# The one-hot table's operations at other places of the attention's steps

## The chip, the cores and the metric

The kernel runs on one core of one Trainium2 chip. The metric is the device time of one execution in microseconds (us), as the median of several runs. The core's engines are named as in the profile: PE (matrix products and transpositions), DVE (vector operations), ACT (activations and copies), POOL (a second vector engine), SP (issues most DMAs). Each engine takes its instructions in the order in which they were written, and waits where a semaphore is not there yet.

## The reference

Eight batches of eight-head attention over 576 positions with head size 64 (four heads with a local mask, four with a strided one) give 4608 rows of 512; each row goes to one of eight experts, the one with the largest gate logit.

```python
scores = np.where(masks, scale * q @ k.T, -1e9)
attn = exp(scores - max) / (sum + 1e-9);  x = (attn @ v) as rows of B*S by 512
logits = x @ w_gate;  e_idx = argmax(logits);  gate_w = softmax(logits)[e_idx]
eom = sigmoid(x @ w_output_gate)
for e in range(8):
    m = e_idx == e
    out[m] = gate_w[m] * eom[m, e] * (relu(x[m] @ w1[e]) @ w2[e])
```

## The kernel before, in words

**The attention** (lines 173 to 888) is a software pipeline of 40 steps: batch b has five chunks of positions, and pass t of the loop brings in chunk t % 5 of batch t // 5. "Step 2" below is a pass with t % 5 = 2. Chunks 0 to 2 are strided, 3 and 4 local. The order on every engine is the order in which this loop writes. One pass does, for chunks of different age: on PE the scores of the new chunk (`scores`, L262 and L267), transpositions of the probabilities of the chunk two passes old (`turn_p`, L320), the products with V of the chunk three passes old (`values`, L335 and L338), and transpositions of the output of the chunk four passes old (`turn_x`, L384). DVE divides the output by its sums (`norm`, L348, L350, L353), then adds the mask to the new scores (`bar`, "the mask" below, L280 and L285) and takes the row maxima (`top`, L294). POOL subtracts the maxima (`shift`, "the subtraction", L309). ACT copies the transposed output of the pass before out of PSUM (`evac_x`, L393, L399), then the transposed probabilities (`evac_p`, L326), V tiles (L233), and last takes the exponential of the new chunk (`expo`, L313). The scores, the products with V and both kinds of transposition have one PSUM buffer each.

**The gate.** When all chunks of a batch are transposed, `logits` multiplies them with the gate's weights in two halves (L416), ACT copies the result (L420), PE transposes it (L425, "the logits' transpositions") and DVE sums it (L427). In the trace the sum of the first half ("the first sum") comes ahead of step 0's division, that of the second ("the second sum") ahead of step 1's mask. `gating` then finds each row's expert (`oh`, one-hot over the experts), counts rows (`cum`), and gives every row a slot: PE forms running numbers (L561 to L566), DVE picks the row's own one (L618) and sums it to `slots` (L621), and `lo` is the slot's low seven bits (L673).

**The one-hot table.** From `lo` and `slots` POOL makes `pos` (L676 to L678) and, with a subtraction from a row of constants, a table `hit` of 128 low numbers and 48 pages for each of six groups of rows: `low` in two pieces (L683), `high` (L686). DVE compares the whole table with zero in place (L691), so that it is one-hot ("the compare"). POOL also splits the row's weight into three bf16 `parts` (L649, L651) and multiplies the pages with five values, two for the row's number and three for the weight, into `named` (L656, "the five products"). Last PE multiplies `hit` with `named` in one PSUM tile (`place`, L662, "the placement"), and DVE adds that to a book of all rows (`enter`, L669; L671 for the first batch).

**What sets the order.** `gating` and `logits` are generators that the pass calls at nine points (`pump(1)` to `pump(9)`). `yield n` lets n further points go by; `yield 0, p` goes on at point p of the same or the next pass. Point 9 stands ahead of the mask, points 1 and 2 in the division, points 3 and 4 behind the subtraction, points 5 to 8 at the end of the pass. Batches 0 to 5 run in this way (`steady`); batches 6 and 7 are worked off in the attention's tail, in the other branch.

After the fourth batch's book entry two more chains begin: `pick` chooses the expert with the most rows, SP loads its number and starts four loads of its first weights (`ahead`, L167), and POOL fetches rows for it (L158), at fixed steps. After the attention's tail the experts follow (lines 890 to 1270), mostly PE products.

Of the kernel before, what the change touches and what calls it, by code (L numbers as in the profile page):

```python
# [20 lines left out]
E = 8  # L21
# [4 lines left out]
R = S // STRIDE  # L26
QB = 96
# [27 lines left out]
HB = CLEAR // 128  # L55
WP = 3
# [4 lines left out]
def attn_moe_kernel(  # L61
# [111 lines left out]
    def attention():  # L173
        with ExitStack() as actx:
# [364 lines left out]
            def gating(b, j0, j1, ci):  # L539
# [12 lines left out]
                def output_logit():  # L552
                    V.tensor_tensor(out=dd[:, 2], in0=oh, in1=l[:, :, E:2 * E], op=ALU.mult)
# [23 lines left out]
                def sigmoid():  # L577
                    nc.scalar.activation(out=f[:, 4, :], in_=f[:, 3, :], func=AF.Exp, scale=-1.0)
# [12 lines left out]
                yield 0  # L591
                if steady:
# [5 lines left out]
                    yield 0, 9  # L598
                    output_logit()
                    yield 0  # L600
                    output_sum()
                    yield 0
                    sigmoid()
                else:
# [10 lines left out]
                V.tensor_tensor(out=cum[0:QB, ci + 1, :], in0=cum[0:QB, ci, :], in1=s8, op=ALU.add)  # L615
                yield 0 if steady else 1
                dst = slots[:, tcols]
                V.tensor_tensor(out=dd[:, 3], in0=pv.rearrange("p (j e) -> p j e", j=n), in1=oh, op=ALU.mult)  # L618
                yield 0
                with nc.allow_low_precision(reason="one slot's number among zeros, written as an integer"):  # L620
                    R(out=dst, in_=dd[:, 3], axis=AX.X, op=ALU.add)  # L621
                yield 0
# [10 lines left out]
                P, last = nc.gpsimd, ci == NC - 2  # L633
                W = V if last else P
                nh = E * HB
                lo = gt.tile([QB, n], I32, name="lo")
                pos = gt.tile([QB, 3, n], F32, name="pos")
                hit = gt.tile([QB, n, 128 + nh], BF16, name="hit")
# [3 lines left out]
                low, high = hit[:, :, 0:128], hit[:, :, 128:128 + nh]  # L642
                many = lambda row, js: row.unsqueeze(1).to_broadcast([QB, js.stop - js.start, row.shape[1]])
                wide = lambda col, m: col.unsqueeze(2).to_broadcast([QB, col.shape[1], m])
# [28 lines left out]
                V.tensor_scalar(out=lo, in0=dst, scalar1=127, scalar2=None, op0=ALU.bitwise_and)  # L673
                if steady:
                    yield 0, 1
                    P.tensor_copy(out=pos[:, 0, :], in_=lo)  # L676
                    P.tensor_copy(out=pos[:, 2, :], in_=dst)
                    P.tensor_tensor(out=pos[:, 1, :], in0=pos[:, 2, :], in1=pos[:, 0, :], op=ALU.subtract)  # L678
# [3 lines left out]
                    for js in (slice(0, JH), slice(JH, n)):  # L682
                        P.tensor_tensor(out=low[:, js], in0=many(lows, js), in1=wide(pos[:, 0, js], 128), op=ALU.subtract)  # L683
                    yield 0, 3
                    V.reciprocal(out=wall[:, tcols], in_=f[:, 5, :])
                    P.tensor_tensor(out=high, in0=many(highs, slice(0, n)), in1=wide(pos[:, 1, :], nh), op=ALU.subtract)  # L686
                    yield 1
                    parted()
                    yield 0, 3
                    yield 0, 2  # L690
                    V.tensor_scalar(out=hit, in0=hit, scalar1=0.0, scalar2=None, op0=ALU.is_equal)  # L691
                    for v in range(1 + WP):
                        name(v)
                    yield 0, 3
                    name(1 + WP)
# [6 lines left out]
                else:  # L702
                    V.tensor_tensor(out=pos[:, 1, :], in0=dst, in1=lo, op=ALU.subtract)
# [730 lines left out]
```

## Time and profile before

| | us |
|---|---|
| median of 3 runs (lowest, highest) | 627.11 (626.43, 628.92) |
| the profiled execution | 632.12 |
| its span on the core | 630.3 |

The profiled execution is 5.0 us above the median, 1.8 us of its 632.12 lie around the span. Busy shares of the span: PE 93%, DVE 50%, ACT 45%, POOL 32%. The page's second part cuts the span into 40 slices of 15.8 us: the attention fills the first nine and a half; DVE stands at 8 tenths from the second to the ninth and the DMA share at 8 or 9 in all nine; from the fourteenth slice on PE stands at 9. The mean granted clock of PE is 0.984. A row of a timeline has the start, the time of one merged group, engine, line, operation, tiles and sizes, and in brackets the engine's idle time before it with what ended that.

### The profile page before, as it was taken

How to read it: one execution, taken by the hardware profiler on the slowest of the kernel's cores; microseconds unless marked ns; L12 is line 12 of the kernel's file. 1: busy time of each engine (PE TensorE's matmuls, PEld its weight loads, DVE VectorE, ACT ScalarE, POOL GpSimd, SP SyncE). 2: the span in 40 equal slices, each digit the busy share in tenths (PEclk: the TensorE clock that was granted, in tenths of full speed). 3: DMA queues.
4: the chain of work that ended last, by engine and by line, in shares of the span. 5: the costliest groups of instructions: out<-in, count | busy, mean ns of one | idle time of the engine just before them, and what ended most of it. 6: DMA issues, size and time to landing. Idle time of an engine off the chain costs nothing. (4 is left out here: it accounts for less than half of the span.)

```text
span 630.3 us, 14983 instructions
## 1 busy us (share of the span) xinstructions
PE 587.7 (93%) x5863; PEld 502.2 (80%) x5863; DVE 315.9 (50%) x741; ACT 281.7 (45%) x567; POOL 199.4 (32%) x285
## 2 busy tenths in 40 slices
PE   7899999887787999999999999999999999999990
PEld 5677777665565988998898899889988988988880
DVE  4888888886578543443143325334533543542500
ACT  3887876766125343334243334334243543443310
POOL 3337766665241423111310140224024124011030
PEclk9999999998799999999999999999999999999996
DMA  9899988884520845234314430543065164161010
GB/s 309 296 315 294 295 289 260 289 283 137 181 63 18 322 160 181 59 112 166 119 47 154 138 128 17 180 128 116 13 219 144 48 217 142 45 217 49 3 42 17
DMA packets 42489, 97.95 MB, mean 155 GB/s; under 512 B 5458, under 2 KB 16346, under 8 KB 42394
## 3 DMA queue, kind: packets, MB, share of 16 engines
q1 hardware_dynamic: 34122, 73.47, 35.7%
q0 software_dynamic: 6864, 19.74, 9.5%
q10 hardware_dynamic: 1408, 3.38, 1.5%
q8 instruction: 72, 1.18, 0.8%
q14 instruction: 23, 0.19, 0.1%
HBM read 77.74 MB, written 20.58 MB: 156 GB/s over the span
## 5 line engine op out<-in xcount | busy, mean ns | idle before, releaser
L1031 PE MATMUL hp<-xl,w1h 128*128 128x256 f32 (+2 forms) x448 | 138.0, 308 | 0.1
L1031 PE MATMUL hp<-xh,w1h 128*128 128x256 f32 (+2 forms) x448 | 138.1, 308 | 0.0
L1031 PE MATMUL hp<-xh,w1l 128*128 128x256 f32 (+2 forms) x448 | 137.9, 308 | 0.0
L1031 PEld LDWEIGHTS hp<-xl,w1h 128*128 128x128 f32 x448 | 84.8, 189 | 1.2 <-DVE xl L966 0.4
L1031 PEld LDWEIGHTS hp<-xh,w1h 128*128 128x128 f32 x448 | 84.8, 189 | 1.2 <-ACT xh L965 0.3
L1031 PEld LDWEIGHTS hp<-xh,w1l 128*128 128x128 f32 x448 | 84.8, 189 | 0.5
L1046 DVE SCALAR_TENSOR_TENSOR hlb<-hp,hhb 128x384 fp32r<-128x384 f32 (+4 forms) x64 | 35.1, 549 | 81.7 <-ACT hf L1045 74.5
L1144 POOL DMA_INDIRECT out_dram<-ys,idx x32 | 32.9, 1027 | 133.3 <-ACT ys L1143 128.8
L1144 POOL DMA_INDIRECT out_dram<-ys,ri x18 | 20.0, 1112 | 172.4 <-ACT ys L1143 169.3
L1043 ACT ACTIVATE hhb<-hp 128x384 fp32r<-128x384 f32 (+4 forms) x64 | 31.1, 485 | 92.7 <-PE hp L1031 87.4
L1057 PE MATMUL yp<-w2h,hhb 128*128 128x512 f32 (+1 forms) x176 | 70.3, 400 | 0.0
L966 DVE TENSOR_TENSOR xl<-tp,xh 128x512 fp32r<-128x512 f32 (+3 forms) x40 | 25.8, 649 | 86.6 <-ACT xh L965 75.4
L1057 PE MATMUL yp<-w2l,hhb 128*128 128x512 f32 (+1 forms) x176 | 68.8, 391 | 0.0
L1057 PE MATMUL yp<-w2h,hlb 128*128 128x512 f32 (+1 forms) x176 | 68.6, 390 | 0.0
L965 ACT CAST xh<-tp 128x512 fp32r<-128x512 f32 (+3 forms) x40 | 22.0, 556 | 100.4 <-PE tp L1019 100.4
L309 POOL TENSOR_TENSOR p_t<-p_t,st 128x512 f32<-128x512 f32 x40 | 42.6, 1065 | 53.8 <-DVE cum L615 15.8
L158 POOL DMA_INDIRECT xg<-xd,idx x40 | 43.3, 1083 | 13.7 <-issue 9.2
L1057 PE MATMUL yp<-w2l,hha 128*128 128x512 f32 x112 | 44.1, 393 | 2.5 <-DVE w2l L966 2.5
L1057 PE MATMUL yp<-w2h,hha 128*128 128x512 f32 x112 | 45.5, 407 | 0.7 <-issue 0.5
L966 DVE TENSOR_TENSOR w1l<-raw,w1h 128x1024 fp32r<-128x1024 f32 x32 | 39.1, 1225 | 12.0 <-ACT w1h L965 11.8
L1143 ACT ACTIVATE ys<-yp,pages 128x512 f32<-128x512 f32 (+1 forms) x36 | 25.0, 694 | 45.0 <-issue 35.5
L1057 PE MATMUL yp<-w2h,hla 128*128 128x512 f32 x112 | 43.7, 390 | 0.0
(209 smaller groups left out, 1102.8 us busy)
## 6 DMA issues: line engine op xcount, KB each, us to landing
raw<-in_moe_w_dram SPq DMA_DIRECT2D x54, 512.0 KB
vst<-in_vs_dram SPq DMA_DIRECT2D x8, 780.0 KB
vlt<-in_vl_dram SPq DMA_DIRECT2D x16, 292.5 KB
q_t<-in_ql_dram SPq DMA_DIRECT2D x8, 576.0 KB
q_t<-in_qs_dram SPq DMA_DIRECT2D x7, 650.0 KB
xd<-x_t SPq DMA_DIRECT2D x80, 54.0 KB
xd<-x_t SPq DMA_DIRECT2D x16, 256.0 KB
raw<-in_moe_w_dram ACTq DMA_DIRECT2D x6, 512.0 KB
```

The costliest lines, as they stand in the source:

```text
L158: nc.gpsimd.indirect_dma_start(out=dst, out_offset=None, in_=src, in_offset=bass.IndirectOffsetOnAxis(ap=idx, axis=0), bounds_check=top, o ...
L309: nc.gpsimd.tensor_tensor(out=p_t, in0=p_t, in1=st, op=ALU.subtract)
L965: nc.scalar.copy(out=hi, in_=src)
L966: nc.vector.tensor_tensor(out=lo, in0=src, in1=f32(hi), op=ALU.subtract)
L1031: nc.tensor.matmul(out=hp[:, 0:n], lhsT=w[:, k, 128 * j:128 * (j + 1)], rhs=x[:, k, 0:n], start=first, stop=(k == KC - 1 and w is w1l))
L1043: nc.scalar.activation(out=hh[:, j, 0:s], in_=hp[:, 0:s], func=AF.Relu)
L1046: nc.vector.scalar_tensor_tensor(out=hl[:, j, 0:s], in0=hp[:, 0:s], scalar=0.0, in1=f32(hh[:, j, 0:s]), op0=ALU.max, op1=ALU.subtract)
L1057: nc.tensor.matmul(out=yp[0:m, :], lhsT=h[:, j, o:o + m], rhs=w[:, j, :], start=(j == 0 and q == 0), stop=(j == FC - 1 and q == 2))
L1143: nc.scalar.activation(out=ys[0:m, 0:n], in_=yp[0:m, 0:n], func=AF.Copy, scale=w[0:m, :])
L1144: i = nc.gpsimd.indirect_dma_start(out=out.rearrange("t (k d) -> (t k) d", k=k), out_offset=bass.IndirectOffsetOnAxis(ap=row, axis=0), in_ ...
```

## The change

For batches 0 to 5 the operations are the same, in number and size; they stand at other places. In step 2 the row's own number, its slot and its low bits (with POOL's three operations on `pos`) come ahead of the mask at point 9; the count and the output logit follow behind the maxima, and the low table behind the subtraction, ahead of the weights' three small operations (`f`). The page table moves up to them, ahead of step 3's subtraction. The compare moves from step 0's division to point 9 of step 4, behind that step's division and ahead of its mask. The first of the five products goes between the subtractions of steps 3 and 4, the other four between those of steps 4 and 0. So the placement, and all that follows on it, comes some points earlier. The other branch only calls the same lines by name.

```diff
                 if steady:
@@
                     pv = numbers()
                     yield 0, 9
+                    own_number()
+                    slot()
+                    low_bits()
+                    P.tensor_copy(out=pos[:, 0, :], in_=lo)
+                    P.tensor_copy(out=pos[:, 2, :], in_=dst)
+                    P.tensor_tensor(out=pos[:, 1, :], in0=pos[:, 2, :], in1=pos[:, 0, :], op=ALU.subtract)
+                    yield 0, 3
+                    count_on()
                     output_logit()
+                    for js in (slice(0, JH), slice(JH, n)):
+                        P.tensor_tensor(out=low[:, js], in0=many(lows, js), in1=wide(pos[:, 0, js], 128), op=ALU.subtract)
                     yield 0
                     output_sum()
                     yield 0
                     sigmoid()
+                    yield 0, 1
...
                 if steady:
-                    yield 0, 1
-                    P.tensor_copy(out=pos[:, 0, :], in_=lo)
-                    P.tensor_copy(out=pos[:, 2, :], in_=dst)
-                    P.tensor_tensor(out=pos[:, 1, :], in0=pos[:, 2, :], in1=pos[:, 0, :], op=ALU.subtract)
                     P.tensor_tensor(out=f[:, 4, :], in0=f[:, 4, :], in1=ones, op=ALU.add)
                     P.tensor_tensor(out=f[:, 2, :], in0=f[:, 2, :], in1=tiny, op=ALU.add)
                     P.tensor_tensor(out=f[:, 5, :], in0=f[:, 2, :], in1=f[:, 4, :], op=ALU.mult)
-                    for js in (slice(0, JH), slice(JH, n)):
-                        P.tensor_tensor(out=low[:, js], in0=many(lows, js), in1=wide(pos[:, 0, js], 128), op=ALU.subtract)
+                    P.tensor_tensor(out=high, in0=many(highs, slice(0, n)), in1=wide(pos[:, 1, :], nh), op=ALU.subtract)
                     yield 0, 3
                     V.reciprocal(out=wall[:, tcols], in_=f[:, 5, :])
-                    P.tensor_tensor(out=high, in0=many(highs, slice(0, n)), in1=wide(pos[:, 1, :], nh), op=ALU.subtract)
-                    yield 1
                     parted()
+                    yield 0, 9
+                    V.tensor_scalar(out=hit, in0=hit, scalar1=0.0, scalar2=None, op0=ALU.is_equal)
+                    name(0)
                     yield 0, 3
-                    yield 0, 2
-                    V.tensor_scalar(out=hit, in0=hit, scalar1=0.0, scalar2=None, op0=ALU.is_equal)
-                    for v in range(1 + WP):
+                    for v in range(1, 2 + WP):
                         name(v)
-                    yield 0, 3
-                    name(1 + WP)
                     yield 8
                     held.append((hit, named, n))
                     wp = place(0, 2 + WP)
```

DVE in step 2, from the division's last operation (`x_t`) to the next pass, second batch's turn. Before:

```order
L353 TENSOR_TENSOR x_t<-xp,rs 128x512
L553 TENSOR_TENSOR dd<-oh,l 96x48
L280 TENSOR_TENSOR p_t<-sp,mask 128x2x2x64 x2
L294 TENSOR_REDUCE st<-p_t 128x8
L556 TENSOR_REDUCE f<-dd 96x6
L615 TENSOR_TENSOR cum<-cum,s_1209 96x8
L618 TENSOR_TENSOR dd<-gp,oh 96x48
L621 TENSOR_REDUCE slots<-dd 96x6
L673 TENSOR_SCALAR lo<-slots 96x6
```

The same place with the change:

```order
L353 TENSOR_TENSOR x_t<-xp,rs 128x512
L606 TENSOR_TENSOR dd<-gp,oh 96x48
L610 TENSOR_REDUCE slots<-dd 96x6
L613 TENSOR_SCALAR lo<-slots 96x6
L280 TENSOR_TENSOR p_t<-sp,mask 128x2x2x64 x2
L294 TENSOR_REDUCE st<-p_t 128x8
L603 TENSOR_TENSOR cum<-cum,s_1216 96x8
L553 TENSOR_TENSOR dd<-oh,l 96x48
L556 TENSOR_REDUCE f<-dd 96x6
```

Own number, slot and low bits went from behind the maxima (`st`) to ahead of the mask (`p_t`), the output logit the other way; the book's addition, which stood in this step's division, now stands in step 1 between two small operations of the gate.

POOL from the subtraction of step 2 to the one of step 0. Before, with the subtractions of steps 3, 4 and 0 in it (the row ahead of these is the subtraction of step 2, then come `pos` and `f`):

```order
L683 TENSOR_TENSOR hit<-hcst,pos 96x3x128 x2
L309 TENSOR_TENSOR p_t<-p_t,st 128x512
L686 TENSOR_TENSOR hit<-hcst,pos 96x6x48
L649 CAST parts<-wall 96x6
L651 TENSOR_TENSOR rest<-wall,parts 96x6
L649 CAST parts<-rest 96x6
L651 TENSOR_TENSOR rest<-rest,parts 96x6
L649 CAST parts<-rest 96x6
L309 TENSOR_TENSOR p_t<-p_t,st 128x512
L656 TENSOR_TENSOR named<-hit,hcst 96x6x48 x2
L656 TENSOR_TENSOR named<-hit,parts 96x6x48 x2
L309 TENSOR_TENSOR p_t<-p_t,st 128x512
```

With the change, from the page table on, with the subtractions of steps 3, 4, 0 and 1:

```order
L701 TENSOR_TENSOR hit<-hcst,pos 96x6x48
L309 TENSOR_TENSOR p_t<-p_t,st 128x512
L673 CAST parts<-wall 96x6
L675 TENSOR_TENSOR rest<-wall,parts 96x6
L673 CAST parts<-rest 96x6
L675 TENSOR_TENSOR rest<-rest,parts 96x6
L673 CAST parts<-rest 96x6
L680 TENSOR_TENSOR named<-hit,hcst 96x6x48
L309 TENSOR_TENSOR p_t<-p_t,st 128x512
L680 TENSOR_TENSOR named<-hit,hcst 96x6x48
L680 TENSOR_TENSOR named<-hit,parts 96x6x48 x3
L309 TENSOR_TENSOR p_t<-p_t,st 128x512 x2
```

The page table moved ahead of step 3's subtraction, one product ahead of step 4's; behind step 0's subtraction nothing is left, where the fifth product stood.

PE at the end of step 0 and the start of step 1. Before:

```order
L384 MATMUL xtp<-ident,x_t 128x128 x4
L425 MATMUL gp<-ident,lg 96x128 x3
L267 MATMUL sp<-kbs_130,q_t 64x64 x16
L320 MATMUL tp<-ident,p_t 128x128 x4
L335 MATMUL xp<-vev,pt 32x130
```

With the change, from the last of the six products of the placement on (they follow on the row `xtp`):

```order
L686 LDWEIGHTS hit
L686 MATMUL gp<-named,hit 128x240
L425 MATMUL gp<-ident,lg 96x128 x3
L267 MATMUL sp<-kbs_130,q_t 64x64 x16
L320 MATMUL tp<-ident,p_t 128x128 x4
```

The placement stood one step later, at the end of step 1 ahead of step 2's scores; now it stands ahead of the logits' transpositions whose sum DVE takes first in step 1's gate.

## Rows read from the trace of the kernel before

**Rows 1.** Busy time by engine in a stretch of the experts (span from:to, length, busy).

```profile
300.00:400.00 100.00, 100.00 (x642) 92.12 (x641) 34.88 (x69) 34.09 (x74) 18.95 (x26) 1.00 0.29 94
```

**Rows 2.** Timeline of POOL: subtraction of step 2, batches' first, fifth and sixth turn.

```profile
47.94 1.04 POOL L309 TENSOR_TENSOR p_t<-p_t,st 128x512 f32<-128x512 f32 x1 [2.18 <-DVE cum L615]
...
119.86 1.04 POOL L309 TENSOR_TENSOR p_t<-p_t,st 128x512 f32<-128x512 f32 x1 [3.53 <-DVE cum L615]
...
139.74 1.04 POOL L309 TENSOR_TENSOR p_t<-p_t,st 128x512 f32<-128x512 f32 x1 [2.76 <-DVE cum L615]
```

**Rows 3.** Timeline of DVE, fourth turn, steps 0 to 4.

```profile
90.78 0.35 DVE L427 TENSOR_REDUCE l<-gp 96x48 f32<-96x192 f32 x1 [0.68 <-PE gp L425]
...
91.36 0.38 DVE L691 TENSOR_SCALAR hit<-hit 96x1056 bf16<-96x1056 bf16 x1
...
94.61 0.34 DVE L427 TENSOR_REDUCE l<-gp 96x48 f32<-96x192 f32 x1
...
95.47 0.59 DVE L586 SCALAR_TENSOR_TENSOR ew<-dd,ecst 96x48 f32<-96x48 f32 x1
...
99.35 0.19 DVE L553 TENSOR_TENSOR dd<-oh,l 96x48 f32<-96x48 bf16 x1
99.47 0.74 DVE L280 TENSOR_TENSOR p_t<-sp,mask 128x256 f32<-128x256 f32 x2
100.25 0.69 DVE L294 TENSOR_REDUCE st<-p_t 128x8 f32<-128x512 f32 x1
...
101.03 0.20 DVE L618 TENSOR_TENSOR dd<-gp,oh 96x48 f32<-96x48 f32 x1
...
101.50 0.67 DVE L673 TENSOR_SCALAR lo<-slots 96x6 int32<-96x6 int32 x1
...
108.24 0.35 DVE L427 TENSOR_REDUCE l<-gp 96x48 f32<-96x192 f32 x1 [0.69 <-PE gp L425]
```

**Rows 4.** Timeline of POOL, the same turn.

```profile
91.81 1.30 POOL L656 TENSOR_TENSOR named<-hit,hcst 96x288 bf16<-96x288 bf16 x2 [0.48 <-DVE hit L691]
...
94.33 1.04 POOL L309 TENSOR_TENSOR p_t<-p_t,st 128x512 f32<-128x512 f32 x1
95.33 0.66 POOL L656 TENSOR_TENSOR named<-hit,parts 96x288 bf16<-96x288 bf16 x1
...
101.10 1.04 POOL L309 TENSOR_TENSOR p_t<-p_t,st 128x512 f32<-128x512 f32 x1 [2.48 <-DVE cum L615]
...
102.79 0.19 POOL L679 TENSOR_TENSOR f<-f,hcst 96x6 f32<-96x6 f32 x1
...
104.94 1.04 POOL L309 TENSOR_TENSOR p_t<-p_t,st 128x512 f32<-128x512 f32 x1
105.94 0.67 POOL L686 TENSOR_TENSOR hit<-hcst,pos 96x288 bf16<-96x288 f32 x1
...
107.76 1.04 POOL L309 TENSOR_TENSOR p_t<-p_t,st 128x512 f32<-128x512 f32 x1
```

**Rows 5.** All low bits and all `ew` by line (count: ns least/median/most, first and last start).

```profile
L673 DVE TENSOR_SCALAR lo<-slots x9: 156/673/675, 48.3 to 177.4; 96x6 int32<-96x6 int32 x7, 96x3 int32<-96x3 int32 x2
...
L586 DVE SCALAR_TENSOR_TENSOR ew<-dd,ecst x9: 151/205/593, 43.0 to 175.0; 96x48 f32<-96x48 f32 x7, 96x24 f32<-96x24 f32 x2
```

**Rows 6.** Timeline of PE, the same turn.

```profile
93.62 0.49 PE L425 MATMUL gp<-ident,lg 128*96 128x128 f32 x3
...
97.37 0.78 PE L662 MATMUL gp<-named,hit 96*128 96x240 bf16 x6
98.08 0.69 PE L267 MATMUL sp<-kbs,q_t 64*64 64x64 f32 x32
...
107.22 0.66 PE L384 MATMUL xtp<-ident,x_t 128*128 128x128 f32 x4
107.71 0.49 PE L425 MATMUL gp<-ident,lg 128*96 128x128 f32 x3
```

**Rows 7.** Timeline of ACT: exponential of step 3.

```profile
106.02 0.63 ACT L313 ACTIVATE p_t<-p_t 128x512 f32<-128x512 f32 x1 [0.85 <-POOL p_t L309]
```

More of the change, by code (lines that the diff above doesn't have):

```diff
@@ L591, in gating, with count_on, own_number, slot @@
                 yield 0
+                P, last = nc.gpsimd, ci == NC - 2
+                nh = E * HB
+                dst = slots[:, tcols]
+                lo = gt.tile([QB, n], I32, name="lo")
+                pos = gt.tile([QB, 3, n], F32, name="pos")
+                hit = gt.tile([QB, n, 128 + nh], BF16, name="hit")
+                low, high = hit[:, :, 0:128], hit[:, :, 128:128 + nh]
+                many = lambda row, js: row.unsqueeze(1).to_broadcast([QB, js.stop - js.start, row.shape[1]])
+                wide = lambda col, m: col.unsqueeze(2).to_broadcast([QB, col.shape[1], m])
+                def count_on():
+                    V.tensor_tensor(out=cum[0:QB, ci + 1, :], in0=cum[0:QB, ci, :], in1=s8, op=ALU.add)
+                def own_number():
+                    V.tensor_tensor(out=dd[:, 3], in0=pv.rearrange("p (j e) -> p j e", j=n), in1=oh, op=ALU.mult)
+                def slot():
+                    with nc.allow_low_precision(reason="one slot's number among zeros, written as an integer"):
+                        R(out=dst, in_=dd[:, 3], axis=AX.X, op=ALU.add)
+                def low_bits():
+                    V.tensor_scalar(out=lo, in0=dst, scalar1=127, scalar2=None, op0=ALU.bitwise_and)
                 if steady:
@@ L614, in gating @@
                     yield 0
[L615 to L622, printed above, removed]
+                    count_on()
+                    yield 1
+                    own_number()
+                    yield 0
+                    slot()
+                    yield 0
                 def weights():
@@ L631, in weights @@
                     yield 0
-                P, last = nc.gpsimd, ci == NC - 2
                 W = V if last else P
[L635 to L638, printed above, removed]
                 named = gt.tile([QB, n, 2 + WP, nh], BF16, name="named")
@@ L641, in gating @@
                 rest = gt.tile([QB, WP, n], F32, name="rest")
-                low, high = hit[:, :, 0:128], hit[:, :, 128:128 + nh]
-                many = lambda row, js: row.unsqueeze(1).to_broadcast([QB, js.stop - js.start, row.shape[1]])
-                wide = lambda col, m: col.unsqueeze(2).to_broadcast([QB, col.shape[1], m])
                 def parted():
@@ L671, in enter @@
                         V.tensor_copy(out=flat, in_=wp)
-                V.tensor_scalar(out=lo, in0=dst, scalar1=127, scalar2=None, op0=ALU.bitwise_and)
                 if steady:
-                    yield 0, 1
-                    P.tensor_copy(out=pos[:, 0, :], in_=lo)
-                    P.tensor_copy(out=pos[:, 2, :], in_=dst)
-                    P.tensor_tensor(out=pos[:, 1, :], in0=pos[:, 2, :], in1=pos[:, 0, :], op=ALU.subtract)
                     P.tensor_tensor(out=f[:, 4, :], in0=f[:, 4, :], in1=ones, op=ALU.add)
@@ L702, in gating @@
                 else:
+                    low_bits()
                     V.tensor_tensor(out=pos[:, 1, :], in0=dst, in1=lo, op=ALU.subtract)
```

## Prediction

> **What bounds the kernel now.** I read the page's slices first, to split the time by stage. In the experts PE is busy for the whole of a stretch of 100 us [rows 1], so whatever the attention ends earlier or later comes out at the end unchanged. The change touches only the attention, so I then read the timelines of DVE, POOL, PE and ACT over one turn of five steps, and measured the turns by the subtraction of step 2.
>
> The first three turns take (101.10 - 47.94) / 3 = 17.72 us [rows 2, 4]; the fourth takes 119.86 - 101.10 = 18.76 and the fifth 139.74 - 119.86 = 19.88, with disturbances that the first three lack. The reader should see two chains in a turn. One is DVE's: from the first sum at 90.78 its rows follow each other without a wait until step 4, and the waits named there are for PE, the last of 0.69 [rows 3]. The other is POOL's: in step 3 its subtraction starts at 104.94, directly behind the low table that began with `f` at 102.79 [rows 4]; ACT's exponential then starts at 106.02, having waited 0.85 for it [rows 7]; behind that in ACT's order stands the copy that PE's transposition at 107.22 needs, then come the logits' transpositions at 107.71 [rows 6] and the next first sum at 108.24 [rows 3]. That is 3.30 us from the start of the subtraction to the sum. Both chains end there almost together, so shortening DVE's alone gains little.
>
> **The holds that the change removes.** `lo` works on 6 numbers and yet takes 0.67: it starts at 101.50 and ends at 102.17, and the subtraction on POOL ends at 102.14 [rows 3, 4]. Its shortest case is 0.156, its median 0.673 [rows 5]. In the same way `ew` ends at 96.06 where the fifth product ends at 95.99, and takes 0.59 against a median of 0.205 [rows 3 to 5]. Ahead of the mask `lo` meets an idle POOL (which waited 2.48 there [rows 4]), and the fifth product is gone from `ew`'s place. DVE saves up to 0.52 and 0.39 in a turn. The compare leaves a busy stretch too, worth 0.2 to 0.4 by its 0.38 [rows 3], and stands in step 4, where DVE waited. So DVE's own work in its chain falls by about a microsecond a turn.
>
> **The chain that it builds.** Three moves work the other way. Own number, slot and low bits stand ahead of the mask, so step 2's subtraction waits for them. The placement stands ahead of the logits' transpositions in step 0, so the second sum waits for it. And the placement needs all five products, which POOL reaches only behind everything that began with step 2's subtraction. That closes a loop of one turn:
>
> - DVE from the second sum to the end of step 2's maxima: 100.25 + 0.69 - 94.61 = 6.33; less 0.39 (`ew`), less 0.12 (the output logit, 99.35 to 99.47, now behind the maxima), plus 0.47 (own number and slot, 101.03 to 101.50), plus 0.16 (`lo` alone) [rows 3, 5]: 6.45. The book's addition is in this stretch before and after.
> - Handover to POOL: 101.10 - 100.94 = 0.16 [rows 3, 4].
> - POOL: three subtractions at 105.94 - 104.94 = 1.00; `f` and the low table 104.94 - 102.79 = 2.15; page table and parts 107.76 - 105.94 = 1.82; five products at (94.33 - 91.81) / 4 = 0.63, 3.15 [rows 4]. Sum 10.12. The three operations on `pos` fall into the wait ahead of the subtraction.
> - Handover to PE: no row shows this one; by the neighbours it is between 0.04 (the exponential behind the subtraction's end at 105.98 [rows 4, 7]) and 0.16; I take 0.10.
> - PE: placement 98.08 - 97.37 = 0.71, then 108.24 - 107.71 = 0.53 from the transpositions' start to the sum [rows 3, 6].
>
> Together 18.07. The compare comes on top: it now starts while POOL has work, and the first product waits for it. Below, nothing (it hides beside the parts); above, its 0.38; I take 0.15, nearer the lower end, since five small operations on POOL stand between. The turn becomes **18.2 us** against 17.72.
>
> **The sum.** Three turns at +0.5 are +1.5. In the first turn no placement is there yet, but its subtraction in step 2 comes later by 0.47 + 0.16 - 0.12 = 0.5. Turns four and five I leave at zero: their 1.0 and 2.2 over a quiet turn can swallow part of the loop, but in the fifth the choice of the first expert comes ahead of step 2's mask, and the first row fetch on POOL stands ahead of the last four products. SP's queue, past which the weights' loads move up, belongs here: the third load now goes ahead of the last batch's second V tile, for which ACT copies wait; I take nothing and bound it by the same 2.2. In the attention's tail the placement's 0.71 comes ahead of the last transpositions, and against it stand a hold like `ew`'s (0.39) and a table addition that leaves the gate's stretch: zero, give or take 0.7. Counts and sizes are unchanged, as are PE's work and the DMAs' bytes. Sum **+2.0**: the profiled execution of 632.12 would become 634.1, and the median of 627.11, 5.0 below it, **629.1**.
>
> **The rivals.**
> - *The products are ready when the placement asks.* Then only its 0.71 delays the second sum: 93.62 + 0.71 + 0.53 = 94.86, 4.08 after the first sum; plus 6.45 and 0.16, plus 1.00 + 2.15 + 0.67 to step 3's subtraction, plus 3.30: 17.8 a turn [rows 3, 4, 6]. For it: the products would have to come only 0.4 sooner. Against: POOL has no gap in the loop. Three turns at +0.1, +0.5 at the start, and half of the 3.0 that turns four and five have over 17.8 swallowed: 627.1 + 0.8 - 1.5 = 626.4; with all 3.0 swallowed 624.9.
> - *The compare and POOL hold each other once.* A small DVE operation that meets a running subtraction ends with it, to 0.03 us, as `lo` shows [rows 3, 4]. If the compare, ready while step 3's subtraction runs, waits for its end in the same way and POOL then stands still for the compare's whole 0.38, the loop is 18.07 + 0.38 = 18.45, three turns at +0.7, the start +0.5: 629.8. For it: the next work on POOL, the parts, is ready by then. Against it: in the rows of before POOL waits for the compare's result, and none shows POOL held by a DVE operation. The Trainium skill (SBUF — State Buffer, "Who interferes with whom") states such a lock of a shared port pair, exclusive for a whole instruction, in both directions, and counts `tensor_scalar` in its fast modes among those that take it; by that rule this rival would be the forecast, at 629.8 instead of 629.1.
> - *All that DVE saves comes through:* 0.7 less in each of five turns, 623.6. Against it: step 3's subtraction started directly behind the low table already.
> - *Slower: the compare takes the place of `lo`.* If the compare, in step 4 ahead of the mask, finds POOL busy not only with the subtraction but with the parts too (1.00 and 1.82 - 0.67 = 1.15), it starts 2.15 behind the subtraction's start; with 0.38, the mask's 0.74, the maxima's 0.69 and 0.16, step 4's subtraction comes after 4.12 instead of 1.00 + 1.15 + 0.63 = 2.78. That is 1.34 more in the loop, 19.4; three turns at +1.7, the fourth +0.6, the start +0.5: 633.3. It decides once the compare starts later than POOL's first cast of the parts; 631 is half of it. For it: `lo` was held to the very end of the subtraction.
> - *The change doesn't do what it says:* `lo` takes 0.67 ahead of the mask as well, because POOL was not what held it. Then the loop has 0.52 more, 18.7, and the sum is 3 x 1.0 + 1.0 = 4.0: 631.1. Against it: the match of the ends to 0.03, and the least of 0.156.
>
> **How the numbers follow.** The forecast has 0.36, the mutual hold 0.13, ready products 0.20, the full saving 0.08, the compare in `lo`'s place 0.17, the unchanged `lo` 0.06. A measurement of this kernel can tell about 0.5% from no change, 3.1 us. Beyond it on the fast side lies the full saving (0.08); on the slow side the last two (0.23); within it the other three (0.69). The range from 624.5 to 633.0 leaves out the full saving and the upper half of the compare in `lo`'s place, and holds the bounds of the tail and of the V tile around 629.1.
>
> **What would show it.** `lo` near 0.16 and `ew` near 0.2 in all turns; step 2's subtractions 18.2 apart in the first three turns; DVE idle ahead of the second sum with PE's transpositions as the releaser, and PE idle ahead of the placement with POOL's last product as the releaser. POOL should run without a gap from step 2's subtraction to step 0's. I am wrong if the turns come below 17.6, if PE's placement follows on the outputs' transposition without a wait, or if the compare takes over 0.8.

## The result and the profile after

The changed kernel takes **632.47 us** at the median of 7 runs (630.13 to 638.67), the kernel before 626.68 (625.24 to 628.92) beside it: a ratio of 1.0086 with a 95% interval from 1.0058 to 1.0114. So it is slower, by about 5 us; the forecast was 2.0 slower. A second set of runs (below) gave 632.48 against 627.73, a ratio of 1.0071 (1.0045 to 1.0096).

First the experts. Busy time by engine in the stretch of [rows 1], in the kernel after:

```profile
300.00:400.00 100.00, 100.00 (x639) 91.67 (x638) 34.65 (x62) 35.05 (x74) 19.97 (x27) 1.00 0.32 103
```

PE is busy for all of it, as before. The time was lost ahead of the experts.

Low bits, `ew` and the compare by line (count: ns least/median/most, first and last start), which answer to [rows 5]:

```profile
L613 DVE TENSOR_SCALAR lo<-slots x9: 165/168/195, 44.8 to 182.1; 96x6 int32<-96x6 int32 x7, 96x3 int32<-96x3 int32 x2
...
L586 DVE SCALAR_TENSOR_TENSOR ew<-dd,ecst x9: 153/197/205, 41.2 to 179.7; 96x48 f32<-96x48 f32 x7, 96x24 f32<-96x24 f32 x2
...
L706 DVE TENSOR_SCALAR hit<-hit x6: 452/620/781, 55.0 to 151.1; 96x1056 bf16<-96x1056 bf16 x6
```

Both old holds are gone: the median of `lo` falls from 0.673 to 0.168, the most of `ew` from 0.593 to 0.205. A new one stands in their place: the compare took 0.38 in [rows 3] and now takes up to 0.78.

The turns, in the timeline of POOL (as [rows 2, 4]), with rows of the one turn that no long wait disturbs:

```profile
69.15 1.04 POOL L309 TENSOR_TENSOR p_t<-p_t,st 128x512 f32<-128x512 f32 x1 [1.23 <-DVE rs L348]
70.15 1.61 POOL L632 TENSOR_TENSOR hit<-hcst,pos 96x384 bf16<-96x384 f32 x2
...
72.94 1.04 POOL L309 TENSOR_TENSOR p_t<-p_t,st 128x512 f32<-128x512 f32 x1
73.93 0.39 POOL L673 CAST parts<-wall 96x6 bf16<-96x6 f32 x1
...
75.34 0.67 POOL L680 TENSOR_TENSOR named<-hit,hcst 96x288 bf16<-96x288 bf16 x1
...
77.61 1.92 POOL L680 TENSOR_TENSOR named<-hit,parts 96x288 bf16<-96x288 bf16 x3
79.49 1.04 POOL L309 TENSOR_TENSOR p_t<-p_t,st 128x512 f32<-128x512 f32 x1
...
87.16 1.05 POOL L309 TENSOR_TENSOR p_t<-p_t,st 128x512 f32<-128x512 f32 x1 [0.89 <-DVE st L294]
```

From step 2's subtraction at 69.15 to step 0's at 79.49 no row has a wait. The turn takes 87.16 - 69.15 = 18.01, against 17.72 before and 18.2 in the forecast.

The same turn on DVE and on PE (as [rows 3, 6]): the compare, the second sum; the outputs' transposition, the placement, the logits' transpositions.

```profile
73.49 0.78 DVE L706 TENSOR_SCALAR hit<-hit 96x1056 bf16<-96x1056 bf16 x1
...
80.72 0.35 DVE L427 TENSOR_REDUCE l<-gp 96x48 f32<-96x192 f32 x1 [0.74 <-PE gp L425]
```

```profile
78.56 0.66 PE L384 MATMUL xtp<-ident,x_t 128*128 128x128 f32 x4
79.58 0.78 PE L686 MATMUL gp<-named,hit 96*128 96x240 bf16 x6 [0.37 <-POOL named L680]
80.19 0.49 PE L425 MATMUL gp<-ident,lg 128*96 128x128 f32 x3
```

The loop that was forecast is there, with the two waits that it asks for: PE waits 0.37 for POOL's last product, and the second sum 0.74 for PE. But 0.3 a turn is not 5 us. Of the other turns of this profile (22.6, 20.2, 19.0 and 20.1) the three of 20 and more hold each a wait of PE of 1.35 to 2.31 us for nothing that the profile shows, so one profile cannot say where the rest went.

### The profile page after: what moved, and what is told of

The parts are those of the page before. It is cut to its first block, busy times and chain, and to the rows that moved or that the text cites. A ratio compares the mean times of both kernels' runs of the same rounds, so it can differ in the third digit from the quotient of the medians.

```text
span 636.9 us, 14981 instructions
## 1 busy us (share of the span) xinstructions
PE 590.1 (93%) x5863; PEld 503.8 (79%) x5863; DVE 314.8 (49%) x741; ACT 281.4 (44%) x567; POOL 200.3 (31%) x285
## 3 DMA queue, kind: packets, MB, share of 16 engines
q0 software_dynamic: 6864, 19.74, 9.4%
## 5 line engine op out<-in xcount | busy, mean ns | idle before, releaser
L1160 POOL DMA_INDIRECT out_dram<-ys,ri x18 | 20.1, 1115 | 173.2 <-ACT ys L1159 170.1
```

Of the source, the lines that this page charges most:

```text
L1160: i = nc.gpsimd.indirect_dma_start(out=out.rearrange("t (k d) -> (t k) d", k=k), out_offset=bass.IndirectOffsetOnAxis(ap=row, axis=0), in_ ...
```

## The experiments

Each ratio below is against the kernel before, run beside it (627.5 to 628.3 at the median), with its 95% interval.

**The placement one step later**, as a test of the loop.

```diff
                     for v in range(1, 2 + WP):
                         name(v)
-                    yield 8
+                    yield 16
                     held.append((hit, named, n))
```

> The change, with the placement (and the book's addition behind it) one step later, behind step 1's output transpositions, as it stands before the change; all else stays moved. The changed kernel takes 632.5 us at the median, the kernel before 626.7. Loop theory (the second sum waits for the placement, and the placement for all five products): the wait goes, a turn without disturbance falls from 18.0 to about 17.1 to 17.5 us, and the time to 624 to 627.5, that is by 5 to 8 us. Queue theory (the loads of the first expert's weights, which the change moves up on SP's queue because the choice of the expert comes a step earlier, take the bandwidth or the buffers): they go back as well, so the time also falls, to 627 to 629, but the quiet turns stay near 18.0. Stall theory (what the change costs are stretches in which PE waits for nothing that the profile shows, 5 us more of them in the turns of the changed kernel's profile than before, and they fall where they fall): the time stays at 631 to 634 with such stretches in the profile as long as in the changed kernel's.

Measured: 631.89, ratio 1.0061 (1.0034 to 1.0087). The quiet turns do fall, to 17.9, 17.9, 17.6 and 17.6, as the loop theory says, and the time does not. But the run does not test the loop by itself, since it has a new wait in the attention's tail; timelines of DVE and of PE there:

```profile
157.74 0.40 DVE L693 TENSOR_TENSOR book<-book,gp 128x240 f32<-128x240 f32 x1 [2.27 <-PE gp L686]
158.06 0.20 DVE L606 TENSOR_TENSOR dd<-gp,oh 96x48 f32<-96x48 f32 x1
```

```profile
156.43 0.66 PE L384 MATMUL xtp<-ident,x_t 128*128 128x128 f32 x4
156.92 0.78 PE L686 MATMUL gp<-named,hit 96*128 96x240 bf16 x6
...
162.26 0.40 PE L335 MATMUL xp<-vev,pt 128*32 128x130 f32 x1 [4.56 <-DVE x_t L353]
```

A pass of the tail has fewer points than one of the loop, so the longer `yield` put the placement of batch 5 behind the next outputs' transposition. The book's addition waits 2.27 for it, ahead of batch 6's own number; the whole table of batch 6 and a division queue behind it on DVE, and PE waits 4.56, where it waits 2.5 to 2.8 in the kernel before and the changed one.

**The first half alone**: numbers, slot, low bits and `pos` early, the rest as before.

```diff
-                    P.tensor_tensor(out=high, in0=many(highs, slice(0, n)), in1=wide(pos[:, 1, :], nh), op=ALU.subtract)
                     yield 0, 3
                     V.reciprocal(out=wall[:, tcols], in_=f[:, 5, :])
+                    P.tensor_tensor(out=high, in0=many(highs, slice(0, n)), in1=wide(pos[:, 1, :], nh), op=ALU.subtract)
+                    yield 1
                     parted()
-                    yield 0, 9
+                    yield 0, 3
+                    yield 0, 2
                     V.tensor_scalar(out=hit, in0=hit, scalar1=0.0, scalar2=None, op0=ALU.is_equal)
-                    name(0)
+                    for v in range(1 + WP):
+                        name(v)
                     yield 0, 3
-                    for v in range(1, 2 + WP):
-                        name(v)
+                    name(1 + WP)
                     yield 8
```

> The change's first half alone: own number, slot, low bits and the three operations on pos ahead of step 2's mask, the low table behind its subtraction; page table, parts, compare, the five products and the placement stand where they stood before. Loop theory: no loop without the early placement; lo takes 0.17 instead of 0.67, ew keeps its 0.59; quiet turns 17.2 to 17.7 us and 624 to 627 in all. Rival (the later subtraction of step 2 is what costs: 0.5 a turn on the path): quiet turns 18.0 to 18.2, 629 to 631. Stall theory: anything from 626 to 632, in step with the sum of the unexplained waits of PE.

Measured: 628.60, ratio 1.0012 (0.9988 to 1.0037); `lo` takes 0.17, a quiet turn 17.5. The time lies between the two ranges that were expected. The hold of 0.5 a turn is gone and no time comes of it; that POOL's subtraction of step 2 comes later by what DVE does ahead of it fits this, but was not tested alone.

**The second half alone**: compare, products and placement early, numbers as before (the edit is to the kernel before).

```diff
                     yield 1
                     parted()
-                    yield 0, 3
-                    yield 0, 2
+                    yield 0, 9
                     V.tensor_scalar(out=hit, in0=hit, scalar1=0.0, scalar2=None, op0=ALU.is_equal)
-                    for v in range(1 + WP):
-                        name(v)
+                    name(0)
                     yield 0, 3
-                    name(1 + WP)
+                    for v in range(1, 2 + WP):
+                        name(v)
                     yield 8
```

> The change's second half alone: slots and low bits stay behind the maxima of step 2 and pos and the low table ahead of step 3's subtraction, but the compare and the first product stand ahead of step 4's mask, the other four products behind step 4's subtraction, and the placement ahead of step 0's transpositions of the logits. Loop theory: the loop is there with lo's hold in it and with page table behind step 3's subtraction; POOL's chain from the pos operations to the last product is some 10.5 us and starts about 0.6 later than in the change, so quiet turns are 18.2 to 18.8 us and the time 632 to 636. Rival (the later subtraction of step 2 is what costs): quiet turns 17.7, 626 to 628. Queue theory: 631 to 633, since the weights' loads are early here too.

Measured: 632.00, ratio 1.0069 (1.0043 to 1.0095), quiet turns 18.2. Nearly the whole loss of the change is in this half.

**The choice of the first expert one step later.**

```diff
                 if ci == EB - 1:
+                    yield 7
                     chains.append([pick(), clock[0] + 1, None])
```

> The change, with the choice of the first expert (and with it the token fetches and the weights' loads) one step later, so that SP's queue has exactly its order of before. Loop theory: nothing changes in the turns, 631 to 634. Queue theory: 627 to 629. Stall theory: 631 to 634 with the same unexplained waits, or, if those come from the early loads' traffic, as the queue theory has it.

Measured: 632.00, ratio 1.0060 (1.0037 to 1.0083). SP's order of the loads costs nothing that can be seen (the changed kernel has 632.47).

**The change in the first four passes, and in the last two.** For these a kernel holds both orders and chooses by batch (`ci`); the four numbers are numbers, products, compare and placement early (1) or as before (0). Only the line that chooses is shown.

```diff
+            modes = lambda ci: (1, 1, 1, 1) if ci < 4 else (0, 0, 0, 0)
```

> The whole change in the first four of the six passes that it touches; in the last two (the ones beside the choice of the first expert, the row fetches and the attention's tail) everything stands as before the change. So far the changed kernel, the change with the late placement and the change's second half alone cost all three some 4.3 to 5.8 us over the kernel before (627.7 in the last runs), and the first half alone 0.9. Turn theory (the loss is spread over the turns: 0.3 to 0.5 in each quiet one): four fifths of it stay, 631 to 632.5. Tail theory (the loss arises where the products stand behind step 4's subtraction beside the row fetches on POOL and where the table's end meets the attention's end): 627 to 629.

```diff
+            modes = lambda ci: (0, 0, 0, 0) if ci < 4 else (1, 1, 1, 1)
```

> The mirror image: the change in the last two of the six passes alone, SP's queue in its order of before. Turn theory: 628 to 629.5. Tail theory: 631 to 633, with the last step-2 subtraction as late as in the quiet turns of the kernel before and the time lost behind it.

Measured: the first four 628.50, ratio 1.0020 (1.0001 to 1.0038); the last two 630.47, ratio 1.0037 (1.0017 to 1.0057). Two thirds of the passes bring 0.8 us, the last third 2.7, just under what the tail theory gave; together that is 3.5 of the 4.8. That speaks for the tail.

**The compare early, the products late.**

```diff
+            modes = lambda ci: (1, 0, 1, 0)
```

> The first half of the change and the compare ahead of step 4's mask (page table behind the low table, parts directly behind step 3's subtraction, as in the change); the five products and the placement stand where they stood before. If the compare in step 4 is what costs (held by step 3's subtraction, it takes 0.78 instead of 0.38 there, and with it the mask and step 4's subtraction come 0.4 later): 630 to 633. If the products behind step 4's subtraction cost: 627 to 629.5, like the first half alone.

Measured: 628.94, ratio 1.0010 (0.9991 to 1.0030), quiet turns 17.4 to 17.8. The held compare costs nothing that can be seen.

**The changed kernel again.**

> The changed kernel as it is, for a second profile and a time on the chip of these runs. Every theory: 631 to 633. Loop theory, as far as it holds: three quiet turns at 18.0 to 18.2, the waits of PE ahead of the placement for POOL's last product in each, and where the first profile of it had turns of 22.6 and 20.2 with waits of PE that nothing explains, this one has others or none; if the same turns are long again, those waits belong to the change.

Measured: 632.48, ratio 1.0071 (1.0045 to 1.0096); turns of 18.7, 18.0, 18.9 and 18.9, so one quiet turn and not three. The turns of 22.6 and 20.2 are not here, so the waits in them come and go with the same kernel. One wait does stay: PE stands 1.64 in the fifth turn, ahead of the same products with V (L338), in both profiles. The tail of this second profile, on PE, and PE's granted clock in it (windows: busy time of PE, PEld, DVE, ACT, POOL, clock, DMA share, GB/s):

```profile
147.24 0.66 PE L384 MATMUL xtp<-ident,x_t 128*128 128x128 f32 x4 [0.33 <-ACT xt L393]
...
152.10 1.28 PE L686 MATMUL gp<-named,hit 96*128 96x240 bf16 x6 [0.92 <-POOL named L680]
153.18 0.84 PE L425 MATMUL gp<-ident,lg 128*96 128x128 f32 x3
153.95 1.15 PE L338 MATMUL xp<-vst,pt 64*64 64x65 f32 x32
155.03 0.92 PE L384 MATMUL xtp<-ident,x_t 128*128 128x128 f32 x4
158.55 0.66 PE L384 MATMUL xtp<-ident,x_t 128*128 128x128 f32 x4
162.96 1.12 PE L384 MATMUL xtp<-ident,x_t 128*128 128x128 f32 x4
166.98 0.60 PE L384 MATMUL xtp<-ident,x_t 128*128 128x128 f32 x4
```

```profile
150.50:155.03 4.53, 3.61 (x49) 2.72 (x46) 1.72 (x5) 1.35 (x4) 1.54 (x3) 0.69 0.16 44
...
162.00:166.98 4.98, 4.40 (x49) 2.40 (x39) 1.06 (x3) 0.98 (x2) 2.01 (x4) 0.66 0.50 137
```

Two suspects stand here. One is the placement, which waits 0.92 for POOL's last product with the logits' transpositions and the outputs behind it. The other is the copy of the last V tile on DVE, which comes later behind the early compare and meets POOL's subtraction (timeline of DVE, then of POOL):

```profile
147.70 1.94 DVE L233 COPY vev<-vlt 64x1040 f32<-64x1040 f32 x1
149.67 0.35 DVE L427 TENSOR_REDUCE l<-gp 96x48 f32<-96x192 f32 x1
```

```profile
147.41 0.67 POOL L680 TENSOR_TENSOR named<-hit,hcst 96x288 bf16<-96x288 bf16 x1
148.04 1.04 POOL L309 TENSOR_TENSOR p_t<-p_t,st 128x512 f32<-128x512 f32 x1
149.04 1.13 POOL L680 TENSOR_TENSOR named<-hit,hcst 96x288 bf16<-96x288 bf16 x1
```

**The last pass's placement back in its old place**, to tell the two apart.

```diff
+            wait = lambda ci: 14 if ci == 5 else 8
...
-                    yield 8
+                    yield wait(ci)
                     held.append((hit, named, n))
```

> The change, with placement and book's addition of its last pass alone put back where the kernel before has them in the attention's tail: behind the first token rows' transpositions instead of ahead of the logits' transpositions. Everything else stays as changed, in that pass too. From the second profile of the changed kernel: in the tail its placement waits 0.92 us for POOL's last product, then runs at the lower clock, and the outputs' transposition behind it comes 7.79 us after the one before it (147.24 to 155.03), against 4.94 where only the first passes are changed (146.57 to 151.51). Tail theory (that wait on PE is where most of the loss of the last passes comes from): 2.9 us come back, 629 to 630. Rival (the copy of the last V tile on DVE, which the compare pushes into step 4's subtraction and which takes 1.94 instead of 0.70 there, is what delays the tail): 631 to 632.5, since the copy stays held.

Measured: 628.79, ratio 1.0023 (0.9999 to 1.0047): 1.3 us over the kernel before, where the changed kernel was 4.8 over it. Its tail on PE, the copy on DVE and the granted clock:

```profile
147.19 0.66 PE L384 MATMUL xtp<-ident,x_t 128*128 128x128 f32 x4 [0.18 <-ACT xt L393]
...
150.04 0.66 PE L493 MATMUL gp<-ident,xg 128*128 128x128 f32 x4 [1.24 <-DVE l L427]
...
150.97 0.49 PE L425 MATMUL gp<-ident,lg 128*96 128x128 f32 x3
151.39 0.70 PE L338 MATMUL xp<-vst,pt 64*64 64x65 f32 x32
152.02 0.66 PE L384 MATMUL xtp<-ident,x_t 128*128 128x128 f32 x4
...
153.38 0.78 PE L713 MATMUL gp<-named,hit 96*128 96x240 bf16 x6
...
156.16 0.66 PE L384 MATMUL xtp<-ident,x_t 128*128 128x128 f32 x4
160.48 0.66 PE L384 MATMUL xtp<-ident,x_t 128*128 128x128 f32 x4
163.45 0.60 PE L384 MATMUL xtp<-ident,x_t 128*128 128x128 f32 x4
```

```profile
147.64 1.96 DVE L233 COPY vev<-vlt 64x1040 f32<-64x1040 f32 x1
```

```profile
150.50:152.02 1.52, 1.52 (x42) 1.27 (x40) 1.01 (x3) 1.04 (x4) 1.51 (x3) 1.00 0.00 0
...
158.50:163.45 4.95, 3.19 (x50) 2.08 (x50) 1.83 (x5) 0.99 (x2) 2.96 (x9) 1.00 0.34 106
```

The copy is held just as long (1.96) and most of the loss is gone (the 1.3 that is left is not clear of noise): the placement was it. The two profiles are alike up to 150.5, so the loss can be read off. From the outputs' transposition at 147 to the next: 155.03 - 147.24 = 7.79 against 152.02 - 147.19 = 4.83, that is 2.96. Of these the wait is 152.10 - 150.97 - 0.05 = 1.08 (0.05 is the difference of the two starts) and the placement up to the transpositions 1.08, of which 0.71 is its length in [rows 6] and the rest the lower clock. The transpositions take 0.77 instead of 0.42 and the outputs 1.08 instead of 0.63, for the clock alone (granted 0.69 against 1.00). The next interval gives 0.62 back, as the placement is gone from it (3.52 against 4.14); the third interval takes 0.09, and the last 1.05, at a clock of 0.66 against 1.00. The sum is 3.48: 1.1 of waiting, 0.1 net of moved work, 2.2 at the lower clock, 0.1 of the rest.

That is one pair of profiles, and of its two large parts the wait comes back in others while the clock's share does not. With the last two passes changed (tail on PE, and its first and last interval in windows):

```profile
149.38 0.78 PE L712 MATMUL gp<-named,hit 96*128 96x240 bf16 x6 [0.93 <-POOL named L706]
```

```profile
144.53:151.04 6.51, 4.36 (x64) 3.18 (x64) 4.49 (x9) 4.41 (x9) 4.79 (x7) 1.00 0.25 75
...
158.84:162.88 4.04, 3.46 (x22) 1.83 (x19) 1.06 (x3) 0.98 (x2) 1.27 (x3) 0.58 0.57 165
```

PE waits as long and goes on at a granted clock of 1.00; the clock falls only in the last interval. With the second half alone PE waits 1.94, again at 1.00. With the choice later it waits 0.93 and the clock falls behind it. In the first profile of the changed kernel PE does not wait for POOL there, and the clock is down already ahead of the placement, where the transpositions that take 0.66 elsewhere (L493) take 1.12 (timeline, then window):

```profile
157.40 1.12 PE L493 MATMUL gp<-ident,xg 128*128 128x128 f32 x4
...
159.16 1.07 PE L686 MATMUL gp<-named,hit 96*128 96x240 bf16 x6
```

```profile
155.36:161.68 6.32, 5.96 (x71) 4.14 (x65) 2.21 (x7) 2.63 (x6) 2.10 (x4) 0.73 0.12 33
```

Over all runs the mean granted clock is 0.9845 for the changed kernel (13 runs) and 0.9862 for the kernel before (102 runs beside the experiments); among these 102 a run with 0.001 less takes some 0.33 us longer. By that the clock would be worth 0.6 of the 4.8 us, an estimate. So the placement in the last pass costs most of the time; how much of it is the wait and how much the clock, beyond this pair, stays open.

**Both together**: the last pass as in the run before, and the placement late in the others too.

```diff
-            wait = lambda ci: 14 if ci == 5 else 8
+            wait = lambda ci: 14 if ci == 5 else 16
```

> As the run with the last pass's placement put back, and in the five passes before it the placement one step later, behind step 1's output transpositions, which takes the loop away there. Loop theory for the first passes and tail theory for the last: both losses gone, 627 to 628.5, within 0.2% of the kernel before. If late placement in the first passes gives nothing: 629 to 630, like the run beside it.

Measured: 627.75, ratio 1.0004 (0.9981 to 1.0027), level with the kernel before. POOL's subtractions of step 2:

```profile
65.37 1.04 POOL L309 TENSOR_TENSOR p_t<-p_t,st 128x512 f32<-128x512 f32 x1 [1.24 <-DVE rs L348]
...
82.91 1.04 POOL L309 TENSOR_TENSOR p_t<-p_t,st 128x512 f32<-128x512 f32 x1 [0.89 <-DVE st L294]
...
100.45 1.04 POOL L309 TENSOR_TENSOR p_t<-p_t,st 128x512 f32<-128x512 f32 x1 [0.89 <-DVE st L294]
...
118.00 1.04 POOL L309 TENSOR_TENSOR p_t<-p_t,st 128x512 f32<-128x512 f32 x1 [0.89 <-DVE st L294]
```

Three turns of 17.54, the second to the fourth, where the run beside it has 18.0, 18.4 and 18.9. At the median that is 1.0 us, but the two intervals overlap, and the 0.8 of the first four passes is no firmer: the two runs without the loop, first half alone and compare early, stand 0.9 and 1.2 over the kernel before. What the loop costs in time is not shown clear of noise.

**An attempt to beat both.** Core of the edit, in batches 0 to 2 and 4:

```diff
+                        yield 0, 3
+                        V.reciprocal(out=wall[:, tcols], in_=f[:, 5, :])
+                        for js in (slice(0, JH), slice(JH, n)):
+                            P.tensor_tensor(out=low[:, js], in0=many(lows, js), in1=wide(pos[:, 0, js], 128), op=ALU.subtract)
+                        yield 0, 3
+                        P.tensor_tensor(out=high, in0=many(highs, slice(0, n)), in1=wide(pos[:, 1, :], nh), op=ALU.subtract)
+                        parted()
+                        yield 0, 2
+                        V.tensor_scalar(out=hit, in0=hit, scalar1=0.0, scalar2=None, op0=ALU.is_equal)
+                        yield 0, 3
+                        for v in range(3):
+                            name(v)
+                        yield 0, 3
+                        for v in range(3, 2 + WP):
+                            name(v)
+                        yield 8
```

> An attempt to beat both, in four of the six passes (first to third and fifth; the others as before the change): own number, slot, low bits and pos ahead of step 2's mask as in the change, but POOL's table work spread over the steps so that no subtraction waits behind it: only the three operations on f ahead of step 3's subtraction, the low table behind it, page table and parts behind step 4's, the compare ahead of step 0's mask, three products behind step 0's subtraction and two behind step 1's, the placement in step 2. If POOL's table work ahead of step 3's subtraction is what keeps a quiet turn at 17.7 (in the changed kernel step 3's subtraction starts 1.4 us after its maxima): quiet turns of 16.8 to 17.3 and 624.5 to 626.5. If DVE's or PE's own chain bounds the turn: 627 to 629.

Measured: 631.61, ratio 1.0052 (1.0026 to 1.0077), above both ranges. Step 3's subtraction now starts 2.95 to 3.16 behind step 2's instead of 3.79, but the quiet turns stay at 17.5 to 18.3, and the turn with the row fetches takes 23.5. POOL's table work ahead of step 3 was not what set the turn; why the fifth turn grew was not tried.

**The kernel before, again.**

> The kernel before, unchanged, for a second profile of its turns and its tail. Tail theory: in the tail its second-last batch's transpositions of the outputs follow each other as in the run where only the first passes are changed: 4.9 us between the last one of the full steps and the first of the tail, against 7.8 in the changed kernel, and some 16 to 16.5 us from there to the last one, against 19.7, unless one of PE's unexplained waits falls into it. Loop theory: quiet turns of 17.4 to 17.9. If instead the tail here is as long as the changed kernel's, the tail theory rests on chance.

Measured: 627.45, ratio 0.9991 (0.9968 to 1.0014), quiet turns 17.5. The distance of the outputs' last transpositions in the tail, from the rows of L384 in each profile (first: the last one of a full step to the next; whole: to the last one):

| kernel | first | whole |
|---|---|---|
| before, first and second profile | 5.08, 4.94 | 17.65, 18.73 |
| first half alone; compare early | 4.80, 4.86 | 16.36, 17.59 |
| first four passes changed | 4.94 | 16.49 |
| last placement back; both late | 4.83, 4.81 | 16.26, 16.24 |
| spread table; placement later | 4.79, 4.81 | 15.86, 20.18 |
| changed, first and second profile | 6.32, 7.79 | 17.09, 19.74 |
| choice later | 7.87 | 20.72 |
| last two passes changed | 6.51 | 18.35 |
| second half alone | 6.95 | 18.97 |

The first interval parts the kernels without exception: 4.8 to 5.1 without the new place of the placement in the tail, 6.3 to 7.9 with it. The whole does not: the run with the placement one step later, which has its own wait, left aside, it goes from 17.1 to 20.7 with the new place and from 15.9 to 18.7 with the old one, since the clock falls in some tails of the kernel before too; my expected 16 to 16.5 was wrong there. At the mean the whole is 18.97 with the new place and 16.90 with the old one, 2.1 apart, so the 3.48 of the pair above is more than the profiles show on average.

## Why the prediction was right and where it was wrong

- **The bound.** That a delay of the attention comes out unchanged at the end held: from the last outputs' transposition to the span's end it is 462.3 to 464.6 over all profiles, with the kernel before at 463.7 and 464.6 and the changed one at 464.4 and 463.8. To about a microsecond either way, then, and no closer.
- **The holds** were right: `lo` at 0.17 to 0.20 and `ew` at 0.15 to 0.21 in all passes, and nothing that can be seen comes of it, as was forecast from both chains ending together.
- **The loop** was right in kind: both waits that it names are in the rows, and POOL has no gap. The quiet turn is 18.01, by the chain's own 18.07, and the nearness is in part luck, for two errors cancel. POOL takes 77.61 + 1.92 - 69.15 = 10.38 instead of 10.12: from the first cast to the first product it is 75.34 - 73.93 = 1.41 instead of 1.15, since the compare holds the cast. So 0.15 for the compare was too little. DVE takes 87.16 - 80.72 = 6.44 with its handover instead of 6.61, and PE 80.72 - 79.53 = 1.19 with its own instead of 1.34. Turns four and five together take 39.0 and 39.4, and 38.6 and 40.2 in the kernel before: zero, as taken. In the time the loop was to be worth 1.5 for three turns and 0.5 at the start; the runs show some 0.8 to 1.0, not clear of noise.
- **The step that failed**, though the time fell into the range, is the tail: "the placement's 0.71 comes ahead of the last transpositions, and against it stand a hold like `ew`'s (0.39) and a table addition that leaves the gate's stretch: zero, give or take 0.7". It is some +3.4: the changed kernel is 4.8 over the kernel before, and 1.3 with only the last pass's placement put back. The prediction set the placement's own length against the savings and left out its wait for the products, though it had priced just that wait for the turns; and it counted no clock. The wait is there in four of the five profiles with the new place (0.92, 0.93, 0.93 and 1.94), and in the pair of profiles it stands on the path in full (1.08). The work behind it ran at the lower clock in two of these four. Without this term the sum of +2.0 is not contradicted: the run with the last placement back measured +1.3, by its interval -0.1 to 2.9.
- **SP's queue** at nothing, bounded by 2.2: with SP's old order the time is 632.00 instead of 632.47, so right as far as can be seen.
- **The rivals.** The compare in the place of `lo` gave 633.3, nearest to 632.5, but not by its mechanism: the compare takes 0.78, is not held through the parts, and the run with it early is at 628.94. The mutual hold exists (last section): it costs POOL 0.26 in the quiet turn, where 0.38 was priced, and no time that can be seen. The full saving did not come. The forecast of +2.0 was 2.8 to 3.8 short, and that the range still held the time is luck: its upper end comes from a rival that did not happen.

## What to carry to other kernels

When an operation moves ahead of another on an in-order engine, price its wait in every stage that runs the same code, and in the drain (the tail) above all: here little was queued to fill the gap, and the clock fell behind it in some of the profiles. Where an order is written with counted yields, the same count lands elsewhere in a loop with fewer points; look up the place in each loop. And before blaming a chain that is visibly there, change it in a part of the passes: that told more here than any single profile.

## What the runs showed of the hardware

- **DVE and POOL hold each other, both ways.** The compare takes 0.78 when it meets step 3's subtraction, and the cast on POOL behind it 0.39, where the other casts of that line take 0.19. The V copy takes 1.94 and the product on POOL behind it 1.13 instead of 0.67. The prediction had seen only POOL holding DVE. The Trainium skill (SBUF — State Buffer, "Who interferes with whom") states such an exclusive lock in either direction, decided by who issues first; these rows agree. Yet the hold of 1.2 us in the tail cost nothing that can be seen, although PE waits behind it: with the last placement back PE stands 1.24 for the sum that follows the copy on DVE (its row at 150.04 above), and where the copy takes 0.70, as with the first four passes changed, it stands as long two operations later, for ACT's copy of the logits:

```profile
150.42 0.53 PE L425 MATMUL gp<-ident,lg 128*96 128x128 f32 x3 [1.22 <-ACT lg L420]
```

The interval is 4.83 with the hold and 4.94 without it.

- **The clock can fall behind a gap on PE, and often does not.** In the tail of the changed kernel's second profile the stretch with the 0.92 wait, and a wait of 1.23 ahead of it, is granted 0.69 on average, so in part the lower of the levels of 1.2 and 2.4 GHz; the same work without the second wait is granted 1.00. With the last two passes changed the same two waits (1.23 and 0.93) stand there, and the whole interval is granted 1.00. It is not the change's alone: the kernel before has such falls in the tails of both its profiles, in the first of them right behind the last full step's transposition (0.54 from 148.96 to 152.45).
- **Waits without a cause.** PE stands for 1.0 to 2.3 us at a time, in all profiles of either kernel, for nothing that the profile shows, and mostly at changing places. They stand in single turns of 20 to 22.6 and hide effects of 0.3; quiet turns and medians of many runs had to be read instead. One belongs to the change: ahead of the products with V in the fifth turn (L338) it is there, with 1.2 to 1.8, in all ten profiles in which that pass has its numbers early, and in none of the other four. No time that can be seen goes with it, as the first half alone and the run with both placements late have it too. What these waits are stays open.
